# One-pass layer norm with ln and exp on ScalarE, k weights in two loads, and a new order for the first tiles of a linear-attention block

## The chip, the cores and the metric

The kernel runs on one core of one Trainium2 chip. The core has five engines, each with its own instruction queue, which it works through in order: TensorE (PE, matrix products), VectorE (DVE), ScalarE (ACT), GpSimd (POOL) and SyncE (SP, which here only issues DMAs). PEld is TensorE's loading of weights, which runs beside its products. Waits between engines go through semaphores. The metric is the device time of one execution in microseconds (us); lower is better.

## The reference

For an input x of 2048 rows by 640 columns in bf16, the reference computes x + A(layernorm(x)) + B(layernorm(x)).

```python
def _layernorm(x, axis=-1, eps=1e-5):
    m = jnp.mean(x, axis=axis, keepdims=True)
    v = jnp.var(x, axis=axis, keepdims=True)
    return (x - m) / jnp.sqrt(v + eps)

def _A_ref(x, wqkv, wo):                      # 32 heads of 20 columns
    q, k, v = ...                             # x @ wqkv, split
    phi = lambda t: jnp.where(t > 0, t + 1, jnp.exp(t)) + 1e-6
    pq, pk = phi(q), phi(k)
    kv = jnp.einsum("bhsd,bhse->bhde", pk, v)
    z = jnp.einsum("bhsd->bhd", pk)
    num = jnp.einsum("bhqd,bhde->bhqe", pq, kv)
    den = jnp.einsum("bhqd,bhd->bhq", pq, z)[..., None] + 1e-6
    return ... (num / den) ... @ wo

def _B_ref(x, w_r, w_gate, w_up, w_down):
    r = x @ w_r                               # one score per row
    idx = jnp.argsort(-r, axis=-1)[:, :C]     # the 8 best rows
    y = (silu(x_sel @ w_gate) * (x_sel @ w_up)) @ w_down
    # y * sigmoid(r_sel) is added to these 8 rows of x
```

## The kernel before, in words

The 2048 rows are 16 tiles (t = 0 to 15) of 128 rows. Every instruction is placed by hand: the order in the source is the order in each engine's queue, and nothing reorders it. PSUM has 8 banks of 512 fp32 columns per partition, written `PS[:, bank, ...]`.

**The stages.** First the tiles go through normalisation, the k projection, phi of k, and the accumulation of G = xn^T · phi(k) over all rows (`G`, with a corner piece in `corner`). G stays in five whole banks and a shared one for all 16 tiles. Then come the q projection in blocks of 512 rows (`q_pe`, `q_fin`), the small products that turn G into the attention's matrix (`kv_pe`, `m_half`), the eight routed rows (`gu_pe` to `y_ev`), the denominators (`den`, `norm`), and the output product per tile (`out_mm`, `out_ev`), whose rows are stored from SP.

**One tile in the first stage.** x arrives in `XX[:, t, 1, :]`. `ln_a` and `ln_b` (L159, L162) take the statistics of the two halves of 320 columns on DVE and `ln_g` (L165) joins them into mean and variance, in bf16. `ln_s` adds eps on DVE (L198) and raises to the power one half on POOL (L199), which gives the standard deviation. `ln_c` computes mean - x into a tile `c`, on DVE (L206) for tiles 0 to 5 and on ACT (L204) for tiles 6 to 15. `ln_xn` takes the reciprocal of the deviation (L211) and multiplies it with `c` (L213); the result is `XX[:, t, 0, :]`. For tiles 1 and 5 the statistics are made otherwise: ACT sums x and its square (L173 to L177) and POOL does the rest (L186 to L193).

The normalised tile is then transposed into `xnT`, five blocks of 128 columns: for tiles 0 to 3 on PE with the identity (L220), three blocks into one bank and two into the next, copied to SBUF by ACT (L224); for tiles 4 to 15 by a DMA that SP issues (`tr_dma`, L229). `K` (L251) multiplies the transposed tile with the k weights in two halves, h = 0 with 320 columns and h = 1 with 321, the last of which is the routing vector w_r. Each half takes five products, one per block of 128. Half h of a tile goes to bank 6 + h, for tile 1 to bank 4 + h. `PHe` and `PHr` (L267, L270) are exp and relu of a half on ACT, `PHb` (L286) joins them into phi(k) on DVE, and `G` (L291, L296) uses it; G waits for all of its tile's phi. POOL sets one column of the normalised tile to ones in between (`ones`, L302).

**The order around the change.** Until tile 3 each step is written out by hand (the "head"); from tile 4 on a loop runs with K of tile t, PHb of t - 1, the normalisation of t + 2 with its DMA transpose, PHe and PHr of t, the statistics of t + 3 and t + 4, and G of t - 1. In the order of PE's queue the head is: products with zeros (L122, L127), which compute nothing that is used, and the transpose of w_r; transposes of 0; K of 0, half 0; transposes of 1; K of 0, half 1; K of 1 around the transposes of 2; K of 2; transposes of 3; G(0); K of 3; G(1); G(2); and then K of 4 and G(3), K of 5 and G(4), and so on.

**Loads.** SP issues, in this order: x of tiles 0, 1 and 2, half 0 of the k weights, x of tile 3, half 1 of the k weights in five pieces, x of tiles 4 and 5, of 6 and 7, of 8 to 11 and of 12 to 15, a DMA transpose of zeros into xnT, two of three copies of a small mask (`bm2`), and then the tile transposes. The k weights lie in one SBUF tile: half 0 as 5 rows of 320 columns and behind it half 1 as 5 rows of 321. The output matrix `Mb` later takes the same memory, with rows of 641 columns.

Of the kernel before, what the change touches and what calls it, by code (L numbers as in the profile page):

```python
# [38 lines left out]
def kernel(  # L39
# [34 lines left out]
    wk = st([P, KC * (D + 1)], BF16, "wk", "wkM")  # L74
# [43 lines left out]
    zero32 = zero[:].bitcast(F32)

    def warm4(n):  # L120
        for _ in range(n):
            pe.matmul(PS[:, 7, :], lhsT=zero32[:, 0:P],  # L122
                      rhs=zero32[:, 0:256].unsqueeze(1).to_broadcast([P, 2, 256]), start=True, stop=True)

    def warm(n, w=512):
        for _ in range(n):
            pe.matmul(PS[:, 7, 0:w], lhsT=zero[:, 0:P], rhs=zero[:, 0:w], start=True, stop=True)  # L127

    pool.memset(halfc[:], 0.5)
    pool.memset(epsb[:], EPS_BF16)  # L130
# [26 lines left out]
    def ln_a(t):  # L157
        sts[t] = tmp.tile([P, 2, nc.vector.BN_STATS_DIM], F32, tag="stats", name="stats", bufs=3)
        dve.bn_stats(out=sts[t][:, 0, :], in_=XX[:, t, 1, 0:320])  # L159
# [23 lines left out]
    msq = st([P, 4], F32, "msq")

    def ln_msq(t):
        pool.tensor_tensor(out=msq[:, 0:1], in0=sm[:, t, 0:1], in1=sm[:, t, 0:1], op=ALU.mult)  # L186

    def ln_var(t):
        pool.tensor_tensor(out=MV[:, t, 1:2], in0=sm[:, t, 1:2], in1=msq[:, 0:1], op=ALU.subtract)
        t2 = tmp.tile([P, 1], BF16, tag="t2", name="t2", bufs=4)  # L190
        ss[t] = tmp.tile([P, 1], BF16, tag="s", name="s", bufs=4)
        pool.tensor_tensor(out=t2[:], in0=MV[:, t, 1:2], in1=epsb[:], op=ALU.add)
        pool.tensor_tensor(out=ss[t][:], in0=t2[:], in1=halfc[:], op=ALU.pow)  # L193

    def ln_s(t):
        t2 = tmp.tile([P, 1], BF16, tag="t2", name="t2", bufs=4)
        ss[t] = tmp.tile([P, 1], BF16, tag="s", name="s", bufs=4)
        dve.tensor_scalar(out=t2[:], in0=MV[:, t, 1:2], scalar1=EPS_BF16, scalar2=None, op0=ALU.add)  # L198
        pool.tensor_tensor(out=ss[t][:], in0=t2[:], in1=halfc[:], op=ALU.pow)  # L199

    def ln_c(t, eng):
        cs[t] = tmp.tile([P, D], BF16, tag="c", name="c", bufs=3)
        if eng is act:
            act.activation(cs[t][:], XX[:, t, 1, :], AF.Identity, bias=MVf[:, t, 0:1], scale=-1.0)  # L204
        else:
            dve.tensor_scalar(out=cs[t][:], in0=XX[:, t, 1, :], scalar1=MVf[:, t, 0:1], scalar2=-1.0,  # L206
                              op0=ALU.subtract, op1=ALU.mult)

    def ln_xn(t, parts=((0, D),)):
        c = cs[t]  # L210
        dve.reciprocal(SR[:, t : t + 1], ss[t][:])  # L211
        for a, b in parts:
            dve.tensor_scalar(out=XX[:, t, 0, a:b], in0=c[:, a:b], scalar1=SR[:, t : t + 1], scalar2=-1.0,  # L213
                              op0=ALU.mult, op1=ALU.mult)

    def tr_pe(t, b0, e0, e1, hs=(0, 1)):
        for b, k0, k1, eng in [((b0, 0, 3, e0), (b0 + 1, 3, KC, e1))[h] for h in hs]:
            pt = PS[:, b, :].bitcast(BF16)[:, 0 : (k1 - k0) * P]
            for kc in range(k0, k1):
                pe.transpose(pt[:, (kc - k0) * P : (kc - k0 + 1) * P], XX[:, t, 0, kc * P : (kc + 1) * P], ident[:])  # L220
            dst = xnT[:, k0:k1, t * P : (t + 1) * P]
            src = pt.rearrange("p (k c) -> p k c", c=P)
            if eng is act:
                act.copy(dst, src)  # L224
            else:
                dve.tensor_copy(dst, src)
# [20 lines left out]
    def K(t, hs=(0, 1), b=6):  # L247
        for h in hs:
            w = HW + h
            for kc in range(KC):  # L250
                pe.matmul(  # L251
                    PS[:, b + h, off(t, h) : off(t, h) + w],
                    lhsT=xnT[:, kc, t * P : (t + 1) * P],
# [693 lines left out]
```

## Time and profile before

| | |
|---|---|
| median of 3 runs | 108.61 us (108.42 to 108.63) |
| the profiled execution | 108.45 us |
| its span in the profile | 106.7 us |
| PE, DVE, ACT, POOL busy | 95%, 79%, 70%, 26% of the span |
| granted TensorE clock | 1.00 throughout |

The profile comes from one execution. A row of the timeline gives the start in us, the duration, the engine, the source line, the operation, what it writes and reads, its shapes, how many instructions of a kind were merged into the row, and in brackets the idle time before it and what ended that. PE's products are pipelined: a row's duration reaches to the end of its last product, which overlaps the start of the next row, so the pace of PE is read from the starts. Rows of groups give busy time, the mean duration of one instruction in ns, and idle time before.

### The profile page before, as it was taken

What the parts mean: (1) busy time and instruction counts of PE and PEld (TensorE: products, weight loads), DVE (VectorE), ACT (ScalarE), POOL (GpSimd) and SP (SyncE); (2) the same over time, 40 slices, a digit from 0 to 9 for tenths busy, and PEclk for the clock granted to TensorE, in tenths of its full rate; (3) what the DMA queues carried; (4) which work ended last, traced back from release to release, by engine and by line L of the source; (5) the groups of instructions that cost most, each with busy time, mean ns of one, the idle gap of its engine ahead of it and who ended that gap; (6) DMA issues with size and microseconds to landing.
All of it is one profiled execution on the core that took longest, in us unless ns stands there. A gap on an engine that the chain in (4) does not pass through costs nothing.

```text
span 106.7 us, 2600 instructions
## 1 busy us (share of the span) xinstructions
PE 101.7 (95%) x923; PEld 62.6 (59%) x923; DVE 84.3 (79%) x207; ACT 74.8 (70%) x163; POOL 27.8 (26%) x79
## 2 busy tenths in 40 slices
PE   5979999999999999999999999999999999999990
PEld 1245656666666666667556545655656677777760
DVE  1789997999998999974898996729598696888870
ACT  4649996888877777888497999997688499200000
POOL 7437235456222222000000593500006200000410
PEclk9999999999999999999999999999999999999999
DMA  2999961435566875889998999901560224796344
GB/s 75 272 276 336 339 82 38 81 74 77 112 141 135 118 138 123 175 219 381 234 399 274 352 339 386 311 26 31 170 237 0 63 95 126 177 364 227 123 126 123
DMA packets 23247, 19.68 MB, mean 184 GB/s; under 512 B 10818, under 2 KB 21698, under 8 KB 23234
## 3 DMA queue, kind: packets, MB, share of 16 engines
q1 hardware_dynamic: 22712, 19.45, 65.5%
q8 instruction: 7, 0.11, 0.4%
q0 software_dynamic: 288, 0.01, 0.4%
q10 hardware_dynamic: 234, 0.06, 0.2%
q14 instruction: 6, 0.05, 0.2%
HBM read 13.80 MB, written 3.65 MB: 164 GB/s over the span
## 4 chain that ended last, share of the span: by engine, by line
PE 84%; DVE 7%; POOL 2%; issue 2%; ACT 1%; DVEq 0%; POOLq 0%
PE PS L502 21%; PE PS L755 19%; PE PS L251 15%; PE PS L291 15%; PE PS L296 3%; PE PS L122 2%; PE PS L678 2%; PE PS L715 2%; DVE XX L213 1%; DVE pk L286 1%; POOL s L199 1%; DVE stats L162 1%; PE PS L566 1%; PE PS L737 1%; PE PS L310 1%
## 5 line engine op out<-in xcount | busy, mean ns | idle before, releaser
L251 PE MATMUL PS<-wk,xnT 128*128 128x320 bf16 (+1 forms) x160 | 24.7, 300 | 0.6 <-ACT xnT L224 0.4
L291 PE MATMUL PS<-pk,XX 128*128 128x512 bf16 x80 | 23.2, 378 | 0.1
L502 PE MATMUL PS<-xnT,wq 128*128 128x512 bf16 x100 | 23.0, 380 | 0.0
L755 PE MATMUL PS<-Mb,pqT 128*128 128x320 bf16 (+2 forms) x165 | 22.1, 295 | 0.0
L251 PEld LDWEIGHTS <-xnT 128*128 128x128 bf16 x160 | 15.4, 98 | 7.4 <-ACT xnT L224 0.9
L755 PEld LDWEIGHTS <-pqT 128*128 128x128 bf16 x165 | 15.8, 97 | 6.4 <-issue 0.2
L267 ACT ACTIVATE ek<-PS 128x320 bf16<-128x320 f32 x32 | 14.3, 446 | 5.2 <-PE PS L251 5.2
L502 PEld LDWEIGHTS <-wq 128*128 128x128 bf16 x100 | 11.3, 118 | 9.0
L557 DVE SCALAR_TENSOR_TENSOR pqT<-qe,qr 128x512 bf16<-128x512 bf16 x20 | 13.5, 683 | 2.0 <-ACT qr L509 1.7
L768 DVE TENSOR_TENSOR o<-PS,XX 128x640 bf16<-128x640 f32 x15 | 12.2, 820 | 3.6 <-PE PS L755 2.8
L508 ACT ACTIVATE qe<-PS 128x512 bf16<-128x512 f32 x20 | 12.2, 609 | 3.8 <-PE PS L502 3.3
L270 ACT ACTIVATE rk<-PS 128x320 bf16<-128x320 f32 x32 | 14.4, 449 | 0.0
L199 POOL TENSOR_TENSOR s<-t,halfc 128x1 bf16<-128x1 bf16 x14 | 8.6, 617 | 21.7 <-DVE t L198 21.7
L296 PE MATMUL PS<-pk,XX 128*128 128x128 bf16 x64 | 14.0, 219 | 0.0
L286 DVE SCALAR_TENSOR_TENSOR pk<-ek,rk 128x640 bf16<-128x640 bf16 x16 | 13.0, 815 | 0.9 <-ACT rk L270 0.7
L291 PEld LDWEIGHTS <-XX 128*128 128x128 bf16 x80 | 7.7, 98 | 8.1
L509 ACT ACTIVATE qr<-PS 128x512 bf16<-128x512 f32 x20 | 12.1, 607 | 0.0
L204 ACT ACTIVATE c<-XX,MVf 128x640 bf16<-128x640 bf16 x10 | 8.4, 839 | 1.7 <-DVE MVf L165 1.6
L241 ACT ACTIVATE XX<-XX,MR,SR 128x640 bf16<-128x640 bf16 x11 | 9.4, 914 | 0.0
L159 DVE BATCH_NORM_STATS2 stats<-XX 128x6 f32<-128x320 bf16 x14 | 6.8, 486 | 1.9 <-DMA XX<-in_A_x_dram 1.9
L213 DVE TENSOR_SCALAR XX<-c,SR 128x640 bf16<-128x640 bf16 (+2 forms) x17 | 6.3, 377 | 1.3
L296 PEld LDWEIGHTS <-XX 128*128 128x128 bf16 x64 | 6.2, 97 | 1.3 <-issue 0.4
(125 smaller groups left out, 104.7 us busy)
## 6 DMA issues: line engine op xcount, KB each, us to landing
out_dram<-o SPq DMA_DIRECT2D x15, 160.0 KB, 2.3
wg<-in_B_w_gate_dram SPq DMA_DIRECT2D x5, 384.0 KB, 8.3
wu<-in_B_w_up_dram SPq DMA_DIRECT2D x5, 384.0 KB, 5.9
wd<-in_B_w_down_dram SPq DMA_DIRECT2D x1, 1920.0 KB, 10.7
XX<-in_A_x_dram SPq DMA_DIRECT2D x2, 640.0 KB, 7.1
wv<-in_A_wqkv_dram SPq DMA_DIRECT2D x5, 160.0 KB, 2.9
wq<-in_A_wqkv_dram SPq DMA_DIRECT2D x1, 800.0 KB, 5.4
hi_d<-XX SPq DMA_DIRECT2D x1, 800.0 KB, 4.5
```

The lines of the kernel that those rows point to most:

```text
L251: pe.matmul(PS[:, b + h, off(t, h) : off(t, h) + w], lhsT=xnT[:, kc, t * P : (t + 1) * P], rhs=wkh[h][:, kc, 0:w], start=(kc == 0), stop=( ...
L267: act.activation(phis[t][0][:, h * HW : (h + 1) * HW], phi_src(t, h, b), AF.Exp)
L270: act.activation(phis[t][1][:, h * HW : (h + 1) * HW], phi_src(t, h, b), AF.Relu)
L286: dve.scalar_tensor_tensor(out=pk[:, t, :], in0=ek[:], scalar=1.0, in1=rk[:], op0=ALU.min, op1=ALU.add)
L291: pe.matmul(PS[:, a, :], lhsT=lhsT, rhs=pk[:, t, 0:512], start=(t == 0), stop=(t == T - 1),)
L296: pe.matmul(PS[:, 5, a * P : (a + 1) * P], lhsT=lhsT, rhs=pk[:, t, 512:D], start=(t == 0 and a == 0), stop=(t == T - 1), skip_group_check= ...
L502: pe.matmul(PS[:, bank, :], lhsT=by5(wq[:, kc, :])[:, m, :], rhs=xnT[:, kc, tb * TBLK : (tb + 1) * TBLK], start=(kc == 0), stop=(kc == KC ...
L508: act.activation(e, PS[:, bank, :], AF.Exp)
L509: act.activation(r, PS[:, bank, :], AF.Relu)
L557: dve.scalar_tensor_tensor(out=pqT[:, m, tb * TBLK : (tb + 1) * TBLK], in0=e, scalar=1.0, in1=r, op0=ALU.min, op1=ALU.add,)
L755: pe.matmul(PS[:, b_, 0 : c1 - c0], lhsT=pqT[:, kc, t * P : (t + 1) * P], rhs=Mb[:, kc, c0:c1], start=(kc == 0), stop=(kc == KC - 1))
L768: dve.tensor_tensor(out=ot[:].rearrange("p (h c) -> p h c", h=2), in0=PS[:, b : b + 2, 0:HW], in1=XX[:, t, 1, :].rearrange("p (h c) -> p h ...
```

## The change

1. `ln_s`, `ln_c` and the path over ACT's sums and POOL (`ln_act`, `ln_msq`, `ln_var`) go. In their place `ln_r` computes exp(-0.5 · ln(variance + eps)) with two instructions of one column on ACT, and `ln_xn` does (x - mean) · that in one pass on DVE, with two per-partition operands. All 16 tiles take their statistics from DVE.
2. The k weights lie in rows of `WS` = 768 columns, half 0 from column 0 and half 1 from column 384; half 1 comes in one load instead of five. `Mb` has rows of 768 too.
3. x of tiles 4 to 15 comes in three loads of four tiles each. All loads of x and the DMA transpose of zeros are issued ahead of everything else in SP's queue.
4. The products with zeros on PE read the constant 0.0 instead of a tile that DVE fills, and are three in fp32, of 512, 256 and 512 columns, instead of two in fp32 of 512 and one in bf16.
5. The copies of `bm2` are made by POOL instead of by DMAs, and together with `bm2` itself early in POOL's queue.
6. A tile's PE transposes are split two and three blocks (`TRP`), as are K's five products (`KA`, `KB`), so that K can begin behind the first two blocks. Copies out of PSUM: the two-block ones on ACT; the three-block ones on DVE, for tile 1 on ACT. The order of the head is new.
7. In the loop `ln_r(t + 3)` stands behind PHe and PHr of t, where `ln_c(t + 3)` stood.

```diff
-    wk = st([P, KC * (D + 1)], BF16, "wk", "wkM")
+    wk = st([P, KC, WS], BF16, "wk", "wkM")
-    wkh = [wk[:, 0 : KC * HW].rearrange("p (k c) -> p k c", k=KC),
-           wk[:, KC * HW : KC * (D + 1)].rearrange("p (k c) -> p k c", k=KC)]
+    wkh = [wk[:, :, 0:HW], wk[:, :, HW + 64 :]]
...
+    ld(sp, wkh[1][:, :, 0:HW], wqkv_v[:, :, D + HW : 2 * D])
+    for a, b in ((4, 8), (8, 12), (12, 16)):
+        ld(sp, XX[:, a:b, 1, :], x_v[:, a:b, :])
+    sp.dma_start_transpose(xnT[:, 0:4, S - P : S], zero[:])
+
+    def warm4(w):
+        pe.matmul(PS[:, 7, 0:w], lhsT=nc.const_aps.tensor(0.0, (P, P), F32),
+                  rhs=nc.const_aps.tensor(0.0, (P, w), F32), start=True, stop=True)
...
-    warm4(1)
+    warm4(512)
+    warm4(256)
     pe.transpose(PS[:, 3, :].bitcast(BF16)[:, 0:KC], wr[:], ident[0:KC, 0:KC])
-    warm4(1)
-    warm(1)
+    warm4(512)
     act.copy(wkh[1][:, :, HW], PS[:, 3, :].bitcast(BF16)[:, 0:KC])
-    for kc in range(KC):
-        ld(sp, wkh[1][:, kc, 0:HW], wqkv_v[:, kc, D + HW : 2 * D])
...
+    def ln_r(t):
+        act.activation(lnv[:, t : t + 1], MV[:, t, 1:2], AF.Ln, bias=eps5[:])
+        act.activation(SR[:, t : t + 1], lnv[:, t : t + 1], AF.Exp, scale=-0.5)
+
+    def ln_xn(t, parts=((0, D),)):
+        for a, b in parts:
+            dve.tensor_scalar(out=XX[:, t, 0, a:b], in0=XX[:, t, 1, a:b], scalar1=MVf[:, t, 0:1],
+                              scalar2=SR[:, t : t + 1], op0=ALU.subtract, op1=ALU.mult)
+    TRP = ((0, 2), (2, KC))
...
-            ld(eng, bm2[32 * g : 32 * g + 32, :], bm2[0:E2, :])
+            pool.tensor_copy(bm2[32 * g : 32 * g + 32, :], bm2[0:E2, :])
...
+    KA, KB = (range(0, 2), range(2, KC))
+    ln_a(0); ln_b(0); ln_a(1); ln_g(0); ln_b(1); ln_r(0); ln_g(1)
+    ln_xn(0, ((0, 2 * P),)); ln_r(1); ln_xn(0, ((2 * P, D),))
+    tr_mm(0, 0, 0); ln_xn(1); tr_cp(0, 0, 0, act); tr_mm(0, 1, 0)
+    ones(0); tr_mm(1, 0, 2); tr_cp(0, 1, 0, dve); K(0, (0,), 6, KA)
+    ln_a(2); tr_cp(1, 0, 2, act); tr_mm(1, 1, 2); ones(1); K(0, (0,), 6, KB)
+    ln_b(2); tr_cp(1, 1, 2, act); K(1, (0,), 4, KA); ln_a(3); PHe(0, 0)
+    K(1, (0,), 4, KB); PHr(0, 0); ln_g(2); ln_b(3); ln_r(2)
+    K(0, (1,), 6, KA); K(1, (1,), 4, KA); ln_g(3); PHe(1, 0, 4)
+    K(0, (1,), 6, KB); ln_xn(2); ln_r(3); tr_mm(2, 0, 0); K(1, (1,), 4, KB)
+    PHe(0, 1); ln_xn(3); tr_cp(2, 0, 0, act); tr_mm(2, 1, 0); ones(2); PHr(0, 1)
+    tr_mm(3, 0, 2); K(2, (0,), 6, KA); tr_cp(2, 1, 0, dve); PHr(1, 0, 4)
+    tr_mm(3, 1, 2); ones(3); PHb(0); K(2, (1,), 6, KA); PHe(1, 1, 4)
+    K(2, (0,), 6, KB); PHr(1, 1, 4); rcopy1(5); tr_cp(3, 1, 2, dve)
+    K(2, (1,), 6, KB); tr_cp(3, 0, 2, act); ln_a(4); PHe(2, 0)
+    G(0, (0, 1, 4, 2, 3)); PHr(2, 0); ln_b(4); PHe(2, 1); ln_g(4); PHb(1)
+    PHr(2, 1); ln_r(4); K(3, (0,), 6, KA); K(3, (1,), 6, KA); ln_xn(4)
+    K(3, (0,), 6, KB); ln_a(5); tr_dma(4); K(3, (1,), 6, KB); ...
...
-                ln_s(t + 3)
-            ln_c(t + 3, act)
+            ln_r(t + 3)
...
-    Mb = st([P, KC, D + 1], BF16, "Mb", "wkM")
+    Mb = st([P, KC, WS], BF16, "Mb", "wkM")
```

The lines of the new head are joined here, several calls to a line; the order is that of the source.

More of the change, by code (lines that the diff above doesn't have):

```diff
@@ L26 @@
 ZD = 4 * P
-ACTS = ()
 TF = 11
+WS = 768
 BF16 = mybir.dt.bfloat16
@@ L115 @@
     ld(sp, XX[:, 3, 1, :], x_v[:, 3, :])
[L118 to L130, printed above, removed]
+    ld(sp, wkh[1][:, :, 0:HW], wqkv_v[:, :, D + HW : 2 * D])
[5 more added lines that the diff above has]
+                  rhs=nc.const_aps.tensor(0.0, (P, w), F32), start=True, stop=True)
+    dve.memset(eps5[:], EPS_BF16)
     pool.memset(ident[:], 0.0)
@@ L183 @@
[L183 to L193, printed above, removed]
@@ L209, in ln_xn @@
[L209 to L226, printed above, removed]
+            dve.tensor_copy(dst, src)
@@ L458 @@
         PHb(t - 1)
-        if t + 3 < T and t < 5 and t + 3 not in ACTS:
+        if t + 3 < T and t < 5:
             ln_a(t + 3)
```

203 lines of the change are left out of this document (100 added, 103 removed).

## The prediction

> **What bounds the kernel now.** I read the page's busy shares and chain first, then busy time by stage, then the first 15 us engine by engine, and last the loads.
>
> ```profile
> span 106.7 us, 2600 instructions
> PE 101.7 (95%) x923; PEld 62.6 (59%) x923; DVE 84.3 (79%) x207; ACT 74.8 (70%) x163; POOL 27.8 (26%) x79
> PE 84%; DVE 7%; POOL 2%; issue 2%; ACT 1%; DVEq 0%; POOLq 0%
> ```
>
> ```profile
> 16.00:40.00 24.00, 24.00 (x172) 15.07 (x171) 21.89 (x66) 19.33 (x45) 8.81 (x29) 1.00 0.56 102
> 40.00:60.00 20.00, 20.00 (x230) 12.32 (x229) 16.07 (x46) 15.99 (x36) 1.34 (x5) 1.00 0.92 266
> 60.00:80.00 20.00, 20.00 (x256) 11.26 (x255) 14.56 (x32) 17.70 (x36) 5.86 (x16) 1.00 0.66 222
> 80.00:100.00 20.00, 20.00 (x160) 13.87 (x159) 16.50 (x24) 9.74 (x15) 2.41 (x1) 1.00 0.48 149
> ```
>
> In the stretches (length, then busy us of PE, PEld, DVE, ACT, POOL, the granted clock, the DMA share, GB/s) PE is busy for all of 16 to 100 us at a clock of 1.00. Relief of DVE, ACT or POOL there is worth nothing by itself. Only three things can move the end: PE reaching this state earlier, a product becoming shorter, or a new stall. So I look at PE's first 15 us.
>
> ```profile
> 1.23 2.07 PE L122 MATMUL PS<-zero 128*128 128x512 f32 x2 [1.23 <-DVE MVf L109]
> 3.35 2.03 PE L122 MATMUL PS<-zero 128*128 128x512 f32 x2
> 5.22 0.38 PE L127 MATMUL PS<-zero 128*128 128x512 bf16 x1
> 5.82 0.48 PE L220 MATMUL PS<-ident,XX 128*128 128x128 bf16 x5 [0.22 <-DVE XX L213]
> 6.73 0.85 PE L251 MATMUL PS<-wk,xnT 128*128 128x320 bf16 x5 [0.43 <-ACT xnT L224]
> 7.70 1.83 PE L251 MATMUL PS<-wk,xnT 128*128 128x321 bf16 x10
> 13.49 1.53 PE L251 MATMUL PS<-wk,xnT 128*128 128x320 bf16 x10
> 15.18 0.38 PE L291 MATMUL PS<-pk,XX 128*128 128x512 bf16 x1
> ...
> 20.45 0.84 PE L251 MATMUL PS<-wk,xnT 128*128 128x320 bf16 x5
> ...
> 28.53 0.30 PE L251 MATMUL PS<-wk,xnT 128*128 128x320 bf16 x1
> ```
>
> Useful work starts with the transposes at 5.82. A full K takes 1.53 in its row; the two half passes at 7.70 take 1.83, so 0.3 is lost in them. K of tile 3 ends its issue at 14.87 (13.49 + 1.53 less 0.15 of overlap), and G(1) starts only at 15.18: 0.3 lost. Before 6.73 another 0.43 is lost. So the head has about 1.0 us of holes plus whatever an earlier start gives, and nothing behind 15.18. The mark I carry through is K of tile 8, at 28.53: behind it both programs ask the same products of PE.
>
> **The change part by part.** The path of tile 0 first.
>
> ```profile
> 3.15 0.50 DVE L159 BATCH_NORM_STATS2 stats<-XX 128x6 f32<-128x320 bf16 x1 [1.92 <-DMA XX<-in_A_x_dram]
> 4.07 0.21 DVE L165 BATCH_NORM_AGGREGATE MVf<-stats 128x2 bf16<-128x12 f32 x1
> 4.38 0.69 DVE L206 TENSOR_SCALAR c<-XX,MVf 128x640 bf16<-128x640 bf16 x2
> 5.24 0.16 DVE L211 RECIPROCAL SR<-s 128x1 f32<-128x1 bf16 x1 [0.16 <-POOL s L199]
> 5.44 0.51 DVE L213 TENSOR_SCALAR XX<-c,SR 128x384 bf16<-128x384 bf16 x2
> ...
> 14.01 0.39 DVE L213 TENSOR_SCALAR XX<-c,SR 128x640 bf16<-128x640 bf16 x1
> ```
>
> ```profile
> 4.56 0.65 POOL L199 TENSOR_TENSOR s<-t,halfc 128x1 bf16<-128x1 bf16 x1 [1.44 <-DVE t L198]
> ```
>
> ```profile
> L270 ACT ACTIVATE rk<-PS 128x320 bf16<-128x320 f32 x32 | 14.4, 449 | 0.0
> L224 ACT COPY xnT<-PS 128x384 bf16<-128x384 bf16 x4 | 1.9, 480 | 1.0 <-PE PS L220 1.0
> L224 ACT COPY xnT<-PS 128x256 bf16<-128x256 bf16 x4 | 1.5, 386 | 0.0
> L574 ACT ACTIVATE lden<-PS,eps 128x256 f32<-128x256 f32 x2 | 1.0, 476 | 1.6 <-PE PS L566 1.6
> L575 ACT ACTIVATE rden<-lden 128x256 bf16<-128x256 f32 x2 | 0.8, 416 | 0.1
> L631 ACT ACTIVATE gl<-ge 1x8 f32<-1x8 f32 x1 | 0.2, 208 | 0.0
> ...
> L286 DVE SCALAR_TENSOR_TENSOR pk<-ek,rk 128x640 bf16<-128x640 bf16 x16 | 13.0, 815 | 0.9 <-ACT rk L270 0.7
> ...
> 0.79 1.28 ACT L107 ACT_TABLE_LOAD   x1 [0.79 <-PEq L931]
> ```
>
> Now: the aggregate ends at 4.28, and the normalise starts at 5.44, 1.16 later, over eps, POOL's power (0.65) and the reciprocal. After: Ln, Exp, normalise. No ln of 128x1 is in the trace. From below, ln of 1x8 takes 0.21; from above, the 128x256 pair takes 0.48 and 0.42. One column is nearest to the 1x8 row; ln with eps as an operand lies 0.06 over exp in the large pair, so I take 0.27 + 0.03 + 0.20 and 0.05 for each hand-over between engines: 0.60. The table is loaded once, at 0.79, and L574 and L575 run ln and exp with it as it is. Against the saving stands that tile 1's first half of statistics (0.41 between starts, 3.15 to 3.56 by L159's row and its follower) is queued before tile 0's aggregate, which now ends at 4.62. Normalising starts at 5.22, 0.22 earlier than now.
>
> The Trainium skill, "ScalarE: Activation LUTs", section "What ACT_TABLE_LOAD costs", has an instruction with immediate operands at 186 ns plus 0.83 ns per element and 93 ns more for each [128,1] pointer operand. By it the pair is about 0.47 to 0.56, an estimate; the rows' 0.50 lies inside, and the upper end would take some 0.2 off the gain worked out below.
>
> PE cannot use all of this. Its zero products start when the engines are released (0.79 by the table load's row) instead of at 1.23, no longer behind DVE's memset, but grow: by the rows, 512 columns take 2.0 at first (1.23 to 3.24) and 1.87 later (3.35 to 5.22), 256 take half, 1.0. With 0.1 for w_r that is 0.8 + 2.0 + 1.0 + 0.1 + 1.87 = 5.75: tile 0's transposes start there, and gain 0.07. The copy then waits for two blocks instead of three and has 256 columns (0.386 instead of 0.48), so K of tile 0 starts at 6.5 instead of 6.73. Earlier than 6.28 it could not be, by the weights:
>
> ```profile
> 2.18 0.43 SPq L104 DMA_DIRECT2D wk<-in_A_wqkv_dram  x1
> 3.23 2.34 SPq L104 DMA_DIRECT2D wk<-in_A_wqkv_dram  x5
> 14.42 1.21 SPq L229 DMA_TRANSPOSE xnT<-XX  x1
> ...
> DMA to landing us min/median/max: 3.2/3.6/4.1
> ...
> xnT<-XX SPq DMA_TRANSPOSE x12, 2.7
> XX<-in_A_x_dram SPq DMA_DIRECT2D x2, 320.0 KB, 3.9
> ...
> 4.00:8.00 4.00, 3.35 (x21) 1.38 (x20) 3.25 (x13) 2.49 (x9) 1.83 (x5) 1.00 0.99 285
> ```
>
> Half 0 lands at 2.18 + 4.1 = 6.28. Of half 1 the fifth piece is issued at 5.14 and lands near 8.5: that is the 0.3 lost in the passes at 7.70. As one load issued at 3.23 it no longer waits for SP, only for bandwidth: 400 KB at 285 GB/s are 1.4 us behind half 0, so 7.7, or 8.3 if the 160 KB of tile 3's x come wholly in between. K of half 1 is first asked for at 8.1, since K of tile 1, half 0, comes ahead of it. In the middle of 7.7 and 8.3 that costs nothing, which I take; every 0.1 behind 8.1 is lost whole. Tiles 4 to 7 land together; 640 KB behind 1440 KB are there by about 10 (today tiles 6 and 7 are issued at 6.3 and take 3.9), and the first statistics of tile 4 come at 11.4. The cover is 1 us.
>
> From here I step all queues through the new order with the paces from start to start, which are the rows' durations less 0.08 to 0.12 of overlap with the next instruction: 0.137 for a K product, 0.06 for a transpose, G 1.3 per tile; on ACT 0.33 for each exp or relu and 0.27 or 0.38 for a copy; on DVE 0.41 for half statistics, 0.35 for a normalise (0.30 and an estimated 0.05 for its second operand), 0.73 for phi. K of tiles 0 and 1 are done at 9.8. Tile 2's K starts at 10.1, set by ACT, where the ln and exp of tiles 2 and 3 stand between the phis. G(0) comes at 11.65, K of 3 at 12.95 (now 13.49), G(1) at 14.3 (now 15.18, as it no longer waits for phi of tile 1). Tile 4's normalise starts at 13.45 (now 14.01), its DMA transpose is issued at 13.95 (14.42) and lands 2.7 later at 16.6; K of 4 wants it at 17.0 (now 17.78). K of 8 comes out at 27.74. The same stepping of today's program gives 28.64 where the trace has 28.53, so the method errs by about 0.1. Gain to the mark: 28.53 - 27.74 = 0.79.
>
> Product length: the five products of half 0 go at 0.136 (20.45's row: 0.84 less 0.30, over four). Ten take 1.53, so the half with 321 columns goes at 0.139. If the odd row length of 641 is the reason, rows of 768 save 0.003 x 5 per tile, 0.11 over tiles 8 to 15; if the 321st column is, nothing. I take 0.1. That `Mb` has the same rows I cost at nothing, with 0.1 as the upper end.
>
> In the loop ACT loses the subtraction and DVE eps and the reciprocal, under a full PE: nothing. The new wait there is Ln for the aggregate, with the next tile's exp queued behind it, and Exp for Ln; by my stepping the DMA transposes from tile 5 on land 1.0 us or more before their K. The copies of `bm2` leave SP (1.3 us of issue ahead of tile 4's transpose, idle then) for POOL, which is done with them at about 5.4; its first wait behind them is the ones column, wanted by G(0) at 11.65. The zero transpose moves ahead of nothing that waits.
>
> Sum: 108.45 (the profiled run) - 0.79 - 0.1 = 107.56. The median stands 0.16 above that run, so 107.7.
>
> **The rivals.** A: POOL holds DVE up. From 3.1 on POOL runs the mask and then three copies, until 5.4, and tile 0's normalise starts at 5.22.
>
> ```profile
> L670 POOL COPY kv<-kv 64x40 bf16<-64x40 bf16 (+1 forms) x8 | 3.2, 405 | 13.6 <-DVE kv L665 13.2
> ```
>
> If it has to wait for one copy of 0.4, it starts at 5.63; stepped on, K of 8 is at 27.98 and the time 107.95. Against it: at 4.38 two subtractions of c ran while POOL's power did, from 4.56, in 0.69, their usual pace. The Trainium skill, "SBUF — State Buffer", section "SBUF: two separate sides", has DVE's fast modes and POOL locking one pair of ports against each other for a whole instruction. By that rule A happens; the trace's overlap at 4.56 shows no such wait.
>
> B: half 1 of the weights lands late, as its last piece does now, at 8.5 or up to 8.7. Everything behind moves by 0.35 to 0.55: 108.0 to 108.3. For it: bandwidth is full (0.99); against: the same bytes, issued 1.9 us sooner.
>
> C: the change doesn't bring what the head shows: the gain is made and lost again at K of 4 to 6, because the transposes land late, for instance as x's last loads still fill the queues. Then 108.4 to 108.8. Against: the transpose of tile 4 has 0.4 us to spare.
>
> D, slower: the ln and exp pair is dear. In the head six of them stand singly or in pairs on ACT's queue between the phis; with 0.1 more for each instruction, 0.2 per pair, K of 8 is 0.6 later. The gain is gone at 0.8 per pair; at 0.95 the time is 109.1. For it: no row of this form, and the 128x256 pair takes 0.92. Against: both 1x8 rows at 0.21.
>
> E, slower: tiles 4 to 7 land behind 12.5 instead of 10, because one load is complete only with its last tile; at 13.0 the stepping gives 109.1.
>
> **How the numbers follow.** My forecast has 0.58 (107.3 to 108.0), A 0.10, B 0.14, C 0.08, D 0.06, E 0.04. Faster by over 0.2% is below 108.4, about what a measurement here can tell from no change: forecast, A and B, 0.82. Same, C: 0.08. Slower, D and E: 0.10. The range ends below at 107.1 (ln and exp at 0.18 each, the fifth of a us from both product lengths, the median no higher than the profiled run) and above at 108.7, which takes in B and most of C.
>
> **What would show it.** Right: the first transposes at 5.7 to 5.8 directly behind zero products; K of 0 at 6.5, with no hole of 0.3 in the passes with 321 columns; G(1) near 14.3; K of 8 near 27.7; DVE's normalise of 640 columns at 0.39 to 0.44; the ln row at 0.2 to 0.27; PE full from there. Wrong: PE waiting for half 1 at 8.1, for ACT's xnT at tiles 2 and 3, or for the transposes at K of 4; DVE's normalise starting late with POOL busy; an ln row over 0.4.

## The result, and the profile after

The changed kernel takes 108.02 us (median of 12 runs, 107.35 to 109.69), the kernel before 108.51 us beside it (12 runs, 108.36 to 108.63). The ratio is 0.9947, with a 95% interval of 0.9929 to 0.9965: faster by half a per cent. A second series of the same two kernels, which is the first experiment below, gave 107.66 us to 108.64 us, a ratio of 0.9924 (0.9902 to 0.9946). The profiled execution of the first series had its TensorE clock halved for a stretch and took 109.69 us, so the profile after is that of the second series: 107.51 us, where the profile before has 108.45.

Head and chain of the changed kernel's page:

```profile
span 105.8 us, 2535 instructions
PE 100.7 (95%) x914; PEld 63.2 (60%) x924; DVE 81.7 (77%) x181; ACT 69.7 (66%) x172; POOL 17.3 (16%) x58
PE 87%; DMA 4%; issue 2%; ACT 1%; DVE 1%; SPq 1%; DVEq 0%
```

The span is 0.9 us shorter. POOL lost ten points of its share and DVE two, and the end did not move for that: PE has 87% of the chain. New in it is DMA with 4%, a single piece, here in the chain in order of time (start, duration):

```profile
2.20 4.30 DMA wk<-in_A_wqkv_dram
```

That is half 0 of the k weights. It lands at 6.50, and from there PE's products make up the chain. Busy time by stage, with the columns named ahead of the prediction's table:

```profile
0.00:4.00 4.00, 3.15 (x6) 1.49 (x7) 1.36 (x7) 1.39 (x2) 3.18 (x14) 1.00 0.47 133
4.00:8.00 4.00, 3.28 (x22) 1.50 (x22) 3.94 (x13) 2.64 (x10) 1.24 (x6) 1.00 1.03 315
8.00:12.00 4.00, 3.94 (x35) 2.71 (x34) 2.94 (x9) 3.94 (x17) 0.20 (x2) 1.00 1.06 379
```

PE is nearly full from 8 us on, where the kernel before still had holes until 15. PE's timeline of the changed kernel:

```profile
3.79 1.13 PE L121 MATMUL PS<-const-float32-0.0 128*128 128x512 f32 x2
5.37 0.98 PE L174 MATMUL PS<-ident,XX 128*128 128x128 bf16 x7 [0.45 <-DVE XX L165]
6.54 0.43 PE L208 MATMUL PS<-wk,xnT 128*128 128x320 bf16 x2 [0.20 <-DMA wk<-in_A_wqkv_dram]
...
6.98 2.27 PE L208 MATMUL PS<-wk,xnT 128*128 128x320 bf16 x15
...
10.17 0.43 PE L208 MATMUL PS<-wk,xnT 128*128 128x320 bf16 x2
...
13.00 1.53 PE L208 MATMUL PS<-wk,xnT 128*128 128x320 bf16 x10
14.37 0.38 PE L248 MATMUL PS<-pk,XX 128*128 128x512 bf16 x1
...
17.04 1.52 PE L208 MATMUL PS<-wk,xnT 128*128 128x320 bf16 x10
...
27.70 1.52 PE L208 MATMUL PS<-wk,xnT 128*128 128x320 bf16 x10
```

A bracket stands where PE was idle for more than 0.15 us; a shorter wait shows only in a row's length, as in the 1.83 of the kernel before. Behind 6.54 no row here has a bracket: the hole in the products with half 1 (the fifteen at 6.98 go through in 2.27) and the one ahead of G(1), which now starts at 14.37 where K of tile 3 ends, are gone. The mark, K of tile 8, moved from 28.53 to 27.70.

The deviation, on ACT and DVE (timelines of these engines, and three groups):

```profile
4.40 0.29 ACT L160 ACTIVATE lnv<-MVf,eps 128x1 f32<-128x1 bf16 x1 [0.32 <-DVE MVf L157]
4.72 0.20 ACT L161 ACTIVATE SR<-lnv 128x1 f32<-128x1 f32 x1
```

```profile
4.17 0.20 DVE L157 BATCH_NORM_AGGREGATE MVf<-stats 128x2 bf16<-128x12 f32 x1
...
4.96 1.04 DVE L165 TENSOR_SCALAR XX<-XX,MVf,SR 128x256 bf16<-128x256 bf16 x3
```

```profile
L165 DVE TENSOR_SCALAR XX<-XX,MVf,SR 128x640 bf16<-128x640 bf16 x15 | 6.7, 445 | 1.0 <-ACT SR L161 1.0
...
L160 ACT ACTIVATE lnv<-MVf,eps 128x1 f32<-128x1 bf16 x16 | 4.8, 300 | 1.4 <-DVE MVf L157 1.2
...
L161 ACT ACTIVATE SR<-lnv 128x1 f32<-128x1 f32 x16 | 3.2, 203 | 0.5
```

From the end of the aggregate (4.37) to the normalise (4.96) are 0.59 us, where the kernel before needed 1.16.

### The profile page after: what moved, and what is told of

Same layout as the page of the kernel before. It is cut to its first block, busy times and chain, and to the rows that moved or that the text cites. A ratio compares the mean times of both kernels' runs of the same rounds, so it can differ in the third digit from the quotient of the medians.

```text
span 108.0 us, 2545 instructions
## 1 busy us (share of the span) xinstructions
PE 102.9 (95%) x924; PEld 64.1 (59%) x924; DVE 81.8 (76%) x181; ACT 70.0 (65%) x172; POOL 17.7 (16%) x58
## 4 chain that ended last, share of the span: by engine, by line
PE 89%; DMA 5%; SPq 1%; issue 1%; DVE 1%; DVEq 0%
PE PS L208 22%; PE PS L468 21%; PE PS L721 19%; PE PS L248 16%; DMA wk<-in_A_wqkv_dram 5%; PE PS L253 3%; PE PS L644 2%; PE PS L681 2%; SPq L103 1%; PE PS L532 1%; PE PS L703 1%; PE PS L651 1%; PE PS L267 1%; PE PS L174 1%; DVE o L731 1%
## 5 line engine op out<-in xcount | busy, mean ns | idle before, releaser
L208 PE MATMUL PS<-wk,xnT 128*128 128x320 bf16 (+1 forms) x160 | 26.3, 312 | 0.7 <-DMA wk<-in_A_wqkv_dram 0.7
L208 PEld LDWEIGHTS <-xnT 128*128 128x128 bf16 x160 | 16.0, 102 | 8.1 <-issue 0.8
L248 PEld LDWEIGHTS <-XX 128*128 128x128 bf16 x80 | 7.7, 98 | 8.1
L151 DVE BATCH_NORM_STATS2 stats<-XX 128x6 f32<-128x320 bf16 x16 | 7.4, 463 | 2.1 <-DMA XX<-in_A_x_dram 2.1
L165 DVE TENSOR_SCALAR XX<-XX,MVf,SR 128x640 bf16<-128x640 bf16 (+2 forms) x17 | 7.3, 434 | 2.2 <-ACT SR L161 2.2
L259 POOL MEMSET XX<- 128x1 bf16 x16 | 1.7, 107 | 37.5 <-DMA xnT<-XX 18.4
L154 DVE BATCH_NORM_STATS2 stats<-XX 128x6 f32<-128x320 bf16 x16 | 7.6, 476 | 0.0
L558 DVE TENSOR_TENSOR pqT<-pqT,R 128x1280 bf16<-128x1280 bf16 x8 | 6.5, 817 | 0.7 <-DMA R<-rd_d 0.7
```

The lines of the kernel that those rows point to most:

```text
L208: pe.matmul(PS[:, b + h, off(t, h) : off(t, h) + w], lhsT=xnT[:, kc, t * P : (t + 1) * P], rhs=wkh[h][:, kc, 0:w], start=(kc == 0), stop=( ...
L248: pe.matmul(PS[:, a, :], lhsT=lhsT, rhs=pk[:, t, 0:512], start=(t == 0), stop=(t == T - 1),)
```

## The experiments

Ratios are to the kernel before, which ran beside each series (medians 108.64, 108.65 and 108.62 us in the three series); they are not the quotients of the medians and differ from them by up to 0.3%. "The last product" is the start of PE's last instruction.

**1. The changed kernel again.** No edit.

> The changed kernel itself once more, since in the profile of it half 0 of the k weights landed at 7.17 (0.9 later than in the kernel before) and PE stood idle long enough ahead of it that its clock fell. Theory W (weights late): also in a profile at full clock K of tile 0 waits for half 0 of the weights, starts at 6.8 to 7.2 instead of the predicted 6.5, and the missing 0.35 us of the gain is this hole. Rival O (order): K of tile 0 starts at 6.5, and the 0.35 us is lost later, in ACT's queue at tiles 2 and 3 or at K of tile 4. Time 0.5 us below the kernel before by both.

Measured: 107.66 us (107.46 to 108.18), ratio 0.9924 (0.9902 to 0.9946). The last product starts at 102.67 instead of 103.63: 0.96 earlier, of which 0.83 was won by the mark at 27.70. Neither theory had that: the 0.35 us that both looked for is not lost in this execution.

**2. Half 1 in five pieces.** The changed kernel with the five loads of the kernel before; x of tiles 4 to 15 moves back 1.9 us in SP's queue.

```diff
-    ld(sp, wkh[1][:, :, 0:HW], wqkv_v[:, :, D + HW : 2 * D])
+    for kc in range(KC):
+        ld(sp, wkh[1][:, kc, 0:HW], wqkv_v[:, kc, D + HW : 2 * D])
```

> The changed kernel with half 1 of the k weights in five pieces again, which puts x of tiles 4 to 15 back by 1.9 us in SP's queue; the layout of 768 columns stays. Theory W in the form that the early loads of x crowd out half 0: half 0 lands at 6.3, K of tile 0 starts at 6.5, but half 1 now lands at 8.5 and costs 0.3 there: about the time of the changed kernel, the hole in another place. If instead the rows of 768 columns slow the load: half 0 lands as late as in the changed kernel, and the time is 0.2 to 0.3 us above it. Rival O: no hole at half 0 in either.

Measured: 108.17 us (107.85 to 110.0), ratio 0.9961 (0.9941 to 0.9980), half a us above the changed kernel. But the profile has the same head: K of tile 8 at 27.71, the last product at 102.68. PE's rows of this run:

```profile
3.79 2.08 PE L122 MATMUL PS<-const-float32-0.0 128*128 128x512 f32 x2
5.66 0.98 PE L175 MATMUL PS<-ident,XX 128*128 128x128 bf16 x7
6.54 0.45 PE L209 MATMUL PS<-wk,xnT 128*128 128x320 bf16 x2
```

The last of the five pieces landed at 8.0, like the one load (8.02). So one load buys no time here, and neither expectation held: the head is the same and the time is not. What differs is the end: from the last product to the end of the span 3.42 us instead of 3.11. Runs 9 to 11 take that up.

**3. Half 0 ahead of x of tile 2.**

```diff
+    ld(sp, wkh[0], wqkv_v[:, :, D : D + HW])
     ld(sp, XX[:, 2, 1, :], x_v[:, 2, :])
-    ld(sp, wkh[0], wqkv_v[:, :, D : D + HW])
```

> The changed kernel with half 0 of the k weights issued ahead of x of tile 2, so that it lands some 0.4 to 0.5 us earlier. Theory W: K of tile 0 starts at 6.5 or little later, and the time is 0.3 to 0.4 us below the changed kernel: 0.85 us below the kernel before, as predicted. Rival O: no difference to the changed kernel within 0.1 us. By both, x of tile 2 lands before its statistics are due at 6.5, or costs up to 0.2.

Measured: 107.85 us (107.53 to 108.34), ratio 0.9928 (0.9904 to 0.9952): no gain. PE's rows:

```profile
3.78 2.08 PE L121 MATMUL PS<-const-float32-0.0 128*128 128x512 f32 x2
5.65 0.99 PE L174 MATMUL PS<-ident,XX 128*128 128x128 bf16 x7
6.54 0.59 PE L208 MATMUL PS<-wk,xnT 128*128 128x320 bf16 x2
...
8.73 1.12 PE L208 MATMUL PS<-wk,xnT 128*128 128x321 bf16 x7 [0.28 <-DMA wk<-in_A_wqkv_dram]
```

K of tile 0 starts at 6.54 again, and not because of the weights: the zero products end 0.94 later in this execution than in run 1's (5.86 instead of 4.92), the transposes start behind them at 5.65, and the copy follows. Half 1 landed at 8.69; its first product starts at 8.73, where in run 1 it was due at 8.13, and K of tile 8 came out at 28.31, 0.6 behind run 1's. At that first product run 3 is 0.60 behind: 0.44 is the wait (the product ahead of it starts at 8.15, and the next could have followed 0.14 later), 0.15 is PE's pace up to 6.9, of which more below. By K of tile 2 (10.64 instead of 10.17) 0.13 of it is made good, and at K of tile 5 0.11 is lost again. There the transposed tile landed at 20.26, just ahead of its K at 20.30. So a late half 1 costs nearly as much as it is late.

**4. The new loads alone.** The kernel before, with half 1 in one load, all x loads ahead, and even row lengths (672) for the k weights and `Mb`; norm and order as before.

```diff
-    wk = st([P, KC * (D + 1)], BF16, "wk", "wkM")
+    wk = st([P, KC, 672], BF16, "wk", "wkM")
...
+    ld(sp, wkh[1][:, :, 0:HW], wqkv_v[:, :, D + HW : 2 * D])
+    for a, b in ((4, 8), (8, 12), (12, 16)):
+        ld(sp, XX[:, a:b, 1, :], x_v[:, a:b, :])
```

> The kernel before with the loads alone of the change: half 1 in one load, x of tiles 4 to 15 in three loads right behind it, k weights and Mb in rows of 672 columns with both halves at even offsets (768 don't fit beside its other tiles). Theory W, early x crowds out half 0: half 0 lands at 6.8 to 7.2 and K of tile 0 starts that much later than its 6.73, while the hole of 0.3 at the fifth piece goes: 108.3 to 108.7, no gain. If the loads don't disturb each other: the hole goes and the odd rows go, 0.3 and 0.2, so 108.0. A K pass with 321 columns goes at 0.136 per product if the odd rows were the reason for 0.139, at 0.139 if the 321st column is.

Measured: 108.97 us (108.84 to 110.76), ratio 1.0039 (1.0014 to 1.0064). PE's row of half 1:

```profile
8.28 1.52 PE L251 MATMUL PS<-wk,xnT 128*128 128x321 bf16 x10 [0.31 <-DMA wk<-in_A_wqkv_dram]
```

In the old order K of tile 0 asks for half 1 early, and now its first product waits 0.31 for the whole load, where it waited before for the last piece. K of tile 8 is 0.14 later than before (28.67). The time is above what either theory gave (108.0, and 108.3 to 108.7), and the hole at half 1 stayed. The last product, though, starts at 103.64, as before, so 0.13 is won behind the mark. Where, the chain's pieces show, each with start, duration and count: ten products of one K in the kernel before, then in this run, then in the changed kernel.

```profile
28.69 1.37 PE PS L251 x10
```

```profile
28.84 1.36 PE PS L251 x10
```

```profile
30.53 1.36 PE PS L208 x10
```

From K of tile 8 to the first output product it is 52.59 us before and 52.51 in both others, and from there to the last product 22.51 and 22.46. The output products have 320 columns, so it isn't the 321st column that cost, but the odd row length (321 for half 1 in the kernel before, 641 for `Mb`): 0.08 us in K and 0.05 with `Mb`. Where the rest of this run's time goes, runs 9 to 11 show.

**5. A dearer pair.** The changed kernel with one more copy of 128x1 on ACT between ln and exp.

```diff
         act.activation(lnv[:, t : t + 1], MV[:, t, 1:2], AF.Ln, bias=eps5[:])
-        act.activation(SR[:, t : t + 1], lnv[:, t : t + 1], AF.Exp, scale=-0.5)
+        act.copy(lnw[:, t : t + 1], lnv[:, t : t + 1])
+        act.activation(SR[:, t : t + 1], lnw[:, t : t + 1], AF.Exp, scale=-0.5)
```

> The changed kernel with a third instruction between ln and exp: a copy of the one column on ACT, which ln_r's exp then reads, some 0.23 us more for each tile's ln and exp. It prices rival D. Theory P (the head is set by the chain through ACT's queue, so each 0.1 us on the pair costs 0.3 us at the end): stepping all queues gives K of tile 8 at 28.6 instead of 27.7, 0.85 us more than the changed kernel: 108.5. Rival theory: the pair stands beside other work and 0.23 us on it costs at most once 0.25 us in the head: 107.9 to 108.0.

Measured: 108.88 us (108.50 to 110.39), ratio 1.0027 (1.0004 to 1.0049). The copy lengthens each pair by 0.23 (starts of ln and exp 0.55 apart instead of 0.32), and the whole gain is gone: K of tile 8 at 28.92, 1.22 behind the changed kernel. PE's waits on the way:

```profile
9.61 0.28 PE L177 MATMUL PS<-ident,XX 128*128 128x128 bf16 x2 [0.28 <-DVE XX L168]
...
20.91 1.26 PE L211 MATMUL PS<-wk,xnT 128*128 128x320 bf16 x8 [0.30 <-DMA xnT<-XX]
```

At tile 2 PE waits for the normalise, and at tile 5 for the DMA transpose, which is issued 0.97 later than in run 1 (17.05 instead of 16.08) and landed at 20.87. In run 1 it landed at 19.57, only 0.13 ahead of its K. Of what one pair grows the mark moves by five times as much, more than the 0.85 that was stepped. So ACT's queue in the first tiles is the second limit of this kernel, close behind PE, and tile 5's transpose a third.

**6. The old deviation.** The changed kernel with eps on DVE, the power on POOL and the reciprocal on DVE in place of ln and exp.

```diff
-        act.activation(lnv[:, t : t + 1], MV[:, t, 1:2], AF.Ln, bias=eps5[:])
-        act.activation(SR[:, t : t + 1], lnv[:, t : t + 1], AF.Exp, scale=-0.5)
+        dve.tensor_scalar(out=t2[:], in0=MV[:, t, 1:2], scalar1=EPS_BF16, scalar2=None, op0=ALU.add)
+        pool.tensor_tensor(out=ss[t][:], in0=t2[:], in1=halfc[:], op=ALU.pow)
...
+            dve.reciprocal(SR[:, t : t + 1], ss[t][:])
```

> The changed kernel with eps on DVE, the power one half on POOL and the reciprocal on DVE in the places of ln and exp; the one-pass normalise, the loads and the new order stay. If the short path of the norm is what lets the new order work (theory P): the path from aggregate to normalise is 0.5 us longer at each of the first tiles and the reciprocal holds DVE's queue: stepping puts K of tile 8 more than 1 us later, up to 4.6 us; the time lies 1 to 4.6 us above the changed kernel, 108.7 to 112.3. If the gain comes from the order and the loads alone: at most 0.3 us above the changed kernel.

Measured: 112.34 us (111.77 to 113.67), ratio 1.0371 (1.0330 to 1.0412). POOL's power as a group, and PE's first waits:

```profile
L167 POOL TENSOR_TENSOR s<-t,halfc 128x1 bf16<-128x1 bf16 x16 | 9.5, 591 | 25.0 <-DVE t L166 24.9
```

```profile
6.52 0.69 PE L182 MATMUL PS<-ident,XX 128*128 128x128 bf16 x5 [0.66 <-DVE t L166]
7.96 0.28 PE L182 MATMUL PS<-ident,XX 128*128 128x128 bf16 x2 [0.75 <-DVE XX L173]
```

DVE stands still while POOL does 0.59 per tile, and PE waits for DVE at every one of the first tiles: K of tile 8 is at 31.86, 4.2 us behind the changed kernel's, and the last product is as much later.

**7. Five times as many copies on POOL.** The three copies of `bm2` made five times over, so that POOL copies from 4.17 to 9.76, under the normalises of tiles 0 to 3.

```diff
-    bm2_copies((1, 2, 3))
+    bm2_copies((1, 2, 3) * 5)
```

> The changed kernel with the three copies of bm2 on POOL made five times over, so that POOL copies from 4.2 to about 9.5 us, across the normalise passes of tiles 0, 1 and 2 on DVE. It tests rival A and the rule on the shared ports. If the two engines shut each other out for whole instructions: normalise passes that meet a copy start or end up to 0.34 us later than 0.45 us after their release, POOL's copies stretch too, and the time is 0.1 to 0.4 us above the changed kernel. If they don't: passes of 0.44 to 0.45 us as before, copies of 0.34, and no change of time within 0.1 us (the ones columns behind the copies are due at 11.6).

Measured: 107.96 us (107.42 to 109.05), ratio 0.9924 (0.9907 to 0.9940), the changed kernel's. POOL's and DVE's rows:

```profile
4.17 5.59 POOL L285 COPY bm<-bm 32x160 bf16<-32x160 bf16 x15
```

```profile
5.12 1.08 DVE L165 TENSOR_SCALAR XX<-XX,MVf,SR 128x256 bf16<-128x256 bf16 x3
...
8.63 0.56 DVE L165 TENSOR_SCALAR XX<-XX,MVf,SR 128x640 bf16<-128x640 bf16 x1 [0.19 <-ACT SR L161]
9.38 0.56 DVE L165 TENSOR_SCALAR XX<-XX,MVf,SR 128x640 bf16<-128x640 bf16 x1 [0.19 <-ACT SR L161]
```

A normalise of 640 columns takes 0.56 under the copies and 0.45 without them; the three at 5.12 take 1.08 instead of 1.04, and the two of tile 0 among them no longer than in run 1. The fifteen copies take 0.318 each, the three of the changed kernel 0.312. So there is a price, 0.11 for a whole pass, and a third of what waiting for one copy would be. It doesn't reach the time. (This execution's own 109.05 us come from elsewhere: half 1 landed at 9.75, and PE waited 1.66 for it. The other seven executions took 107.42 to 108.94.)

**8. The norm alone.** The kernel before, with ln and exp, the one pass on DVE, and DVE's statistics for tiles 1 and 5; loads, rows and order of PE's queue as before.

```diff
-    ln_s(0)
-    ln_msq(1)
-    ln_c(0, dve)
-    ln_c(1, dve)
+    ln_r(0)
+    ln_a(1)
+    ln_b(1)
+    ln_g(1)
...
-    ln_s(3)
+    ln_r(3)
...
-    ln_c(3, dve)
```

> The kernel before with part 1 alone: ln and exp on ACT and the one-pass normalise for all tiles, statistics of tiles 1 and 5 on DVE; order of PE, loads, rows and zero products as before. Theory P: in the old order ln and exp of tiles 2 to 4 stand in ACT's queue ahead of the phis that PE waits for; stepping gives K of tile 3 at 14.7 (13.5 in the kernel before) and K of tile 8 at 29.4 instead of 28.5 to 28.6: 109.2 to 109.4, slower than the kernel before. If the shorter path and the relief of DVE are worth something by themselves: 108.2 to 108.6.

Measured: 109.86 us (109.66 to 110.31), ratio 1.0100 (1.0086 to 1.0115): slower by 1%. ACT's rows and the one of PE that waits longest:

```profile
10.37 0.52 ACT L228 ACTIVATE ek<-PS 128x320 bf16<-128x320 f32 x1
10.70 0.52 ACT L231 ACTIVATE rk<-PS 128x320 bf16<-128x320 f32 x1
11.02 0.53 ACT L228 ACTIVATE ek<-PS 128x320 bf16<-128x320 f32 x1
11.34 0.54 ACT L231 ACTIVATE rk<-PS 128x320 bf16<-128x320 f32 x1
...
11.69 0.41 ACT L169 ACTIVATE lnv<-MVf,eps 128x1 f32<-128x1 bf16 x1
12.14 0.20 ACT L170 ACTIVATE SR<-lnv 128x1 f32<-128x1 f32 x1
```

```profile
12.88 0.45 PE L181 MATMUL PS<-ident,XX 128*128 128x128 bf16 x5 [1.00 <-DVE XX L174]
```

In the old order tile 3's ln and exp stand behind four exp and relu passes on ACT; tile 3's aggregate was ready at 8.84, and ln starts at 11.69. The power on POOL had no such queue ahead of it. The normalise comes at 12.4, PE waits a whole us for it, and K of tile 8 is at 30.32.

**9 to 11. The number of DMAs.** The tail of run 2 has a suspect: a DMA of SP or ACT signals its landing on one of eight semaphores, which are handed out in turn, and SP's last waits go through these eight in a fixed order, 0.06 us each. In the kernel before (90 DMAs) and in the changed one (82) the last store's semaphore is the last in that order; in run 2 (86) it is the third, and four more waits follow (the expectation of run 9 has five); in run 4 (85) it is the second, and five follow. Runs 9 and 10 add four loads of 8 bytes to the changed kernel and to run 2's, run 11 adds five to run 4's; they are issued in the middle, near 70 us, and nothing reads them.

```diff
     hi_copy()
+    dum = st([1, 4, 4], BF16, "dum")
+    for k in range(4):
+        ld(sp, dum[:, k, :], B_w_r.rearrange("(kc p) -> kc p", p=P)[0:1, 0:4])
```

> The changed kernel with four loads of 8 bytes more on SP's queue, issued in the middle of the program (near 70 us, where SP is idle); nothing reads them. Theory T (the end of the program is set by an order: SP's last waits go through the DMAs' eight semaphores in a fixed order, 0.06 us each, and each DMA takes the next semaphore in turn): the last store sits on another semaphore, five more waits follow its landing, the last PE product stays at 102.7 and the span grows by 0.3 to 106.1, the time by 0.3. Rival (the 0.3 us of the run with five pieces comes from its loads, for instance from stores that land later): no change, 105.8, ratio 0.992 to the kernel before.

> The run with half 1 in five pieces, and the same four small loads more, so that it has eight DMAs more than the changed kernel. Theory T: the last store is on the same semaphore as in the changed kernel again, the tail behind the last product is 3.1 us again instead of 3.4, and the time is 0.3 below that of the five pieces alone: ratio 0.992 to the kernel before, the same as the changed kernel. Rival: 0.996 as without the small loads.

> The kernel before with the new loads and rows alone, and five small loads more in the middle, so that it has as many DMAs as the kernel before. Theory T: the tail is 3.1 us again instead of 3.48; the last product stays at 103.6 and the time is that of the kernel before within 0.1 us (ratio 1.000 instead of 1.004). Rival: 1.004 stays.

| kernel | DMAs | last product starts | end of span | between | median us |
|---|---|---|---|---|---|
| before | 90 | 103.63 | 106.73 | 3.10 | 108.62 |
| changed (run 1) | 82 | 102.67 | 105.78 | 3.11 | 107.66 |
| changed and four (run 9) | 86 | 103.35 | 106.76 | 3.41 | 108.17 |
| five pieces (run 2) | 86 | 102.68 | 106.10 | 3.42 | 108.17 |
| five pieces and four (run 10) | 90 | 102.88 | 105.99 | 3.11 | 107.87 |
| new loads (run 4) | 85 | 103.64 | 107.12 | 3.48 | 108.97 |
| new loads and five (run 11) | 90 | 103.81 | 106.98 | 3.17 | 108.73 |

The ratios are 0.9947 (0.9931 to 0.9963), 0.9926 (0.9906 to 0.9946) and 1.0009 (0.9992 to 1.0026). All three tails came out as the order of the waits has it: four DMAs more cost 0.3 us, four more on top of them give it back. It is the tails that show it: the medians alone would not, as the changed kernel's own two series (108.02 and 107.66) differ by as much. SP's waits for the last stores, run 1 and run 9 (in total, times, longest):

```profile
SPq L908 <- DMA out_dram<-o: 0.5, 2, 0.3
```

```profile
SPq L911 <- DMA out_dram<-o: 1.0, 2, 0.8
```

Run 9's 0.8 is SP standing at a late store's semaphore before it goes on to the others. So the five pieces cost nothing by themselves (0.9926 against 0.9924), nor do the new loads and rows alone (1.0009). Run 9's profile shows one more thing:

```profile
8.92 1.12 PE L208 MATMUL PS<-wk,xnT 128*128 128x321 bf16 x7 [0.70 <-DMA wk<-in_A_wqkv_dram]
```

Half 1, the same load at the same place in the queue as in run 1, landed at 8.87 here, and the last product is 0.68 later. With the longer tail that makes the 0.98 by which this execution's span exceeds run 1's.

No run was faster than the changed kernel.

## Why the prediction was right, point by point

| step | before | predicted | run 1 |
|---|---|---|---|
| aggregate to normalise, tile 0 | 1.16 | 0.60 | 0.59 |
| normalise of tile 0 starts | 5.44 | 5.22 | 4.96 (5.15 in run 2) |
| zero products end | 5.6 | 5.75 | 4.92 (in runs 2 and 3 the transposes start behind them at 5.66 and 5.65) |
| K of tile 0 | 6.73 | 6.5 | 6.54 |
| half 0 lands | 6.28 | 6.28 | 6.50 |
| half 1 lands | | 7.7 to 8.3 | 8.02 |
| x of tiles 4 to 7 lands | | 10 | 10.01 |
| K of tile 2 | 10.53 | 10.1 | 10.17 |
| K of tile 3 | 13.49 | 12.95 | 13.00 |
| G(1) | 15.18 | 14.3 | 14.37 |
| transpose of tile 4 issued | 14.42 | 13.95 | 13.99 |
| K of tile 4 | 17.78 | 17.0 | 17.04 |
| tile 5's transpose lands ahead of its K by | 0.12 | 1.0 or more | 0.13 |
| K of tile 8 | 28.53 | 27.74 | 27.70 |
| shorter products | | 0.1 | 0.13 |
| the profiled execution | 108.45 | 107.56 | 107.51 |

- **The mark.** Stepping all queues with the paces from start to start gave the head from K of tile 0 on to within 0.1 us; ahead of it, and in the cover of tile 5's transpose, it was off by more. Runs 5, 6 and 8 change the norm's path in three ways, and each time the last product moves with the mark (by 1.22 with 1.22, by 4.16 with 4.16, and by 1.84 with 1.79 in run 8 against the kernel before). That the gain is made in the head and kept is shown.
- **The pair.** Ln was taken at 0.27 and takes 0.30, exp at 0.20 and takes 0.20. The Trainium skill, "ScalarE: Activation LUTs", section "What ACT_TABLE_LOAD costs", has about 280 ns for an instruction with one pointer operand and 187 without, for one column; the rows' 300 and 203 agree to within 20 ns. The prediction gave no row for the 0.05 that it put on the normalise for its second operand; 640 columns take 0.445, and took 0.387 in the pass of the kernel before.
- **The zero products** were mis-sized for run 1 (4.92, not 5.75) and right for runs 2 and 3; why is told below. K of tile 0 is at 6.54 either way, once held by half 0 (6.50), once by the zeros. So that run 1's 6.54 agrees with the predicted 6.5 is in part luck: the zeros and the normalise were early, and half 0 was 0.22 later than its 6.28. That there are two limits so close together was not seen: half 0 was carried as a bound with 0.2 to spare, and there was no room.
- **Product length.** An odd row length is the reason (run 4), though half 1's rows had 321 columns and only `Mb`'s the 641 that the prediction names; and `Mb`, costed at nothing with 0.1 as the upper end, gives 0.05 of the 0.13.
- **Rival A** (POOL holds DVE): 0.11 for a pass of 640 columns, and no effect on the time with five times the copies. The Trainium skill, "SBUF — State Buffer", section "SBUF: two separate sides", has the ports locked for a whole instruction; the rows of run 7 show DVE up to 25% slower while POOL's copies run back to back, not one waiting out the other. Whether these passes run in the mode that takes the lock, no row tells.
- **Rival B** (half 1 lands late) is what was underestimated. The step read "in the middle of 7.7 and 8.3 that costs nothing", with a chance of 0.14 for the other case. In run 1 half 1 landed at 8.02 and cost nothing, and in runs 5 and 6 (8.01 and 7.82) it cost nothing either. In other executions of the same order of loads it landed at 8.87 (run 9) and 9.75 (run 7), and the last product came 0.68 and 1.55 later than in run 1: nearly all of it was lost. In the first series' profiled execution it landed at 8.75, but nothing waited for it. There half 0 was late, at 7.17, PE waited 0.71 for it, and with the clock halved its first product with half 1 started only at 10.09. The 0.3 by which the first series' median (108.02) exceeds 107.7 has the size of such losses; that late loads are its cause is argued from the profiled executions, since the timed ones show no landings. Why the same load is up to 1.9 us later in some executions stays open.
- **Rival C** didn't happen: behind 6.54 no product of the head waited, and K of tiles 4 to 6 wasn't held up. But the prediction had the transposes from tile 5 on land 1.0 us or more ahead of their K. From tile 6 on they do (1.19 for tile 6 in run 1); tile 5's takes 3.5 us from issue to landing instead of the 2.7 that was stepped, and lands 0.13 ahead. Why that one takes longer stays open.
- **Rival D** has the right mechanism and the wrong price. The prediction put the point from which it decides at 0.8 per pair; run 5 has 0.23 more than the 0.52 of the changed kernel, which is 0.75, and there the gain is gone and another 0.2 us with it (108.88 against 108.65). It does move faster than was stepped: 1.22 at the mark for 0.23, where "0.2 per pair" was 0.6, and 0.30 of it is the wait for the DMA transpose of tile 5, which the stepping had with 1.0 to spare.
- **Rival E**: tiles 4 to 7 landed at 10.01 and their first statistics came at 11.48.
- **The parts.** The norm alone is 1.0% slower, the loads and rows alone change nothing (once the number of DMAs is the same), and the order with the old deviation is 3.7% slower; together they are 0.5 to 0.8% faster. The order is worth something only with a short path from the aggregate to the normalise, and ln and exp only where the order puts them ahead of ACT's long passes. The zero products and the place of POOL's first copies weren't tried by themselves.

## What to carry to other kernels

In a kernel whose main engine is full from some point on, step every queue up to that point and compare one mark; what a change does to other engines behind it was worth nothing here. When work moves from an idle engine to one with a queue, what counts is what stands ahead of it in that queue, so move it and reorder together. Leave slack at the transfer on which the first useful work waits: this head has none, and each late landing is paid nearly whole.

## What the runs showed of the hardware that was not expected

- **The number of DMAs** moves the end by 0.3 to 0.4 us (runs 2, 4 and 9 to 11), by the place of the last store's semaphore in the order of the closing waits. Two versions whose numbers of DMAs differ by other than a multiple of eight can differ by that too.
- **Odd row lengths of a product's moving operand** cost a little: products of half 1 start 0.139 us apart with rows of 321, and 0.137 apart with rows of 672 or 768 (means over tiles 4 to 15). With `Mb`, that is 0.13 us from K of tile 8 to the last product.
- **TensorE starts at half its pace, and the granted clock that the views print doesn't show it.** The same zero product took 2.08 in runs 2 and 3 and 1.13 in run 1, with a granted clock of 1.00 in 0 to 8 us of run 1. The doubling came near 4 us there and behind 6 us in runs 2 and 3. The trace's records of the clock begin only with it: at 3.75 in run 1, at 6.49 and 6.88 in runs 2 and 3, and at 5.21 in the kernel before. The views print 1.00 for the time ahead of the first record too, so the "1.00 throughout" given for the kernel before is read from 5.21 on, and the 1.87 that the prediction took for the last zero product is one at half pace. The Trainium skill, "TensorE: Matmul & The Clock Gate", section "Part 1: The HAM clock gate", has a clock halved until one window of 3.4 us was busy, with windows that run free of the kernel's start; the traces agree: their first records begin between 3.75 and 7.13 (run 7's trace has none), and each lasts a multiple of 3.41. The first series' profiled execution has the way back. Stages and PE's timeline of it:

```profile
4.00:8.00 4.00, 2.65 (x15) 1.18 (x16) 3.65 (x12) 1.81 (x7) 1.13 (x5) 0.91 1.02 301
8.00:12.00 4.00, 4.00 (x25) 2.53 (x24) 1.68 (x6) 2.89 (x10) 0.10 (x1) 0.66 1.07 379
```

```profile
5.51 0.99 PE L174 MATMUL PS<-ident,XX 128*128 128x128 bf16 x7 [0.56 <-DVE XX L165]
7.21 0.64 PE L208 MATMUL PS<-wk,xnT 128*128 128x320 bf16 x2 [0.71 <-DMA wk<-in_A_wqkv_dram]
...
7.96 3.56 PE L208 MATMUL PS<-wk,xnT 128*128 128x320 bf16 x15
```

Half 0 landed at 7.17 there. After idle times of 0.56 and 0.71 the fifteen products took 3.56 instead of 2.27, and 0.09 and 0.34 of two stretches of 4 us are 1.72 us of clock lost, which is half of 3.4 us: one window at half clock, and the trace's record has it from 7.31 to 10.72. An idle time of 1.66 at 8.1 in run 7 brought no such stretch (its products behind it take 0.30 each, the usual length), so the length of the hole alone doesn't decide; what does stays open.
